# An S4 convolution beside a gated feed-forward: tables by quarters and one half mixed early, in place of tables by halves and one mixing stage

## The chip, the cores and the metric

The kernel runs on one core of one Trainium2 chip. Its time is the device time of one execution in microseconds (us). Five engines work side by side, each through its own list of instructions in a fixed order: TensorE (PE in the profile, with its weight loads as PEld), VectorE (DVE), ScalarE (ACT), GpSimd (POOL) and SyncE (SP). An engine stops at an instruction whose inputs are not there yet, and everything behind it in its list waits with it. SP computes nothing; it issues all the transfers, and it too stops at a transfer that isn't ready.

## The reference

Two branches read the same input x of 2048 rows by 640 channels and are blended by a gate per row.

```python
g = _sigmoid((x * gate_w).sum(-1, keepdims=True))
a = _A_ref(x, ...)         # long convolution, per channel, plus u * Dskip
b = (_gelu(x @ w_gate) * (x @ w_up)) @ w_down      # 640 -> 1728 -> 640
return g * a + (1 - g) * b

# inside _A_ref, D = 640 channels, N = 128 states, L = 2048
P = jnp.exp(logdA[:, :, None] * l[None, None, :])
K = jnp.einsum("dn,dnl,dn->dl", Cc, P, dB).real
y = irfft(rfft(u, 2 * L) * rfft(K, 2 * L))[:L]
```

So the kernel K(d, l) of every channel has to be made first, a sum of 128 complex exponentials; then u and K are transformed, multiplied and transformed back. The branch b is three matrix products.

## The kernel before

**Feed-forward.** Two groups of 1024 rows. For each of 14 slices of the hidden width, `gate` does ten matmuls of 512 columns (line 500) into a pair of PSUM banks and ACT takes the GELU (504); `up` does ten more (520) and DVE multiplies (524). `downs` does 28 matmuls of 320 columns for 128 rows (548) and scales the result into `zt` (245 on ACT, 249 on DVE). PSUM has eight banks and every step takes two, so four steps can be open at a time.

**The tables of K.** K is factored over two grids of time steps. `kgen(q)` fills two tables for a half of 320 channels, q = 0 or 1: `exps1` (599) and `exps2` (627) take exponentials on ACT, 64 and 40 in all over both halves; `phases` makes angles on DVE (580 scales for the first grid, 582 for the second, 584 adds a quarter turn) and sines on ACT (589); `grid1` and `grid2` multiply both on DVE (613, 614, 637). `cs1` and `cs2` exist once, so the second half's exponentials wait until `contract` has read the first half's tables on PE (650). The contraction's output is evicted, re-sorted by `pick` (661) and stored to the scratch `dS`. `gathers` (744, 752) then brings K back from `dS` in 17 strided transfers into `Kl`.

**The transforms.** A transform of length 4096 is split 64 by 32. The first step (128-row matmuls) is line 719 for u and `stageA`, line 780, for K; both store to DRAM scratch, `dU` and `dKA`. The second step reads the scratch by 32 slots in chunks of four (`loadB`) and uses 64-row tiles: `stageB` (807). `swap` makes a copy of U with real and imaginary rows exchanged by two transfers; `mix` runs stage B on K, multiplies both by U (826, 827) and goes back with 834, then stores to `dY`. `finish` loads dY, does the last step (854), adds with the gate's weight into `zt` (859) and stores the output. `evac` is the helper that copies PSUM to SBUF, on ACT (243) or DVE (247).

In this kernel u's second step, `mix` and `finish` run on all 640 channels at once. `stageA` runs by halves. So no chunk of `mix` can begin before K of both halves is made, and no load of `finish` before the last dY store.

**What sets the order.** `Plan.add` records every step with what it reads and writes. `emit` goes through the list `ORDER`; each number holds the step, its engine and its PSUM pair, and each engine gets its instructions in that order. Nothing is decided at run time. The numbers in P, and the durations given to `add`, have no effect on what is emitted.

Of the kernel before, what the change touches and what calls it, by code (L numbers as in the profile page):

```python
# [27 lines left out]
    336 1392 652 276 12 296 356 436 616 476 636 948 516 24 376 416 316 456 496 964 556 536 44 596 1468 576 224 676  # L28
    696 64 896 936 856 2740 1448 876 396 984 6316 796 1484 816 916 836 1408 716 736 1544 2981 2836 776 756 1064 1428
    2862 3076 1004 1024 1044 4383 2956 2768 1124 1084 1104 2888 10580 10604 3008 4404 2782 10636 1508 3020 2804 2856  # L30
    1568 1604 2903 3096 248 3044 88 3101 2976 4428 1664 2602 1148 6320 3196 6348 2624 2924 1168 6362 2656 3220 6436
    6388 1524 1188 6416 3128 3463 3316 3248 4444 3142 1584 3556 3488 1628 3261 3216 3164 1204 6440 1688 3336 6483
    3822 3284 6556 6464 6508 1644 3501 1228 3916 6536 3848 3340 3576 1244 1264 4183 1284 3368 3436 3524 1704 6562
    4208 4276 6600 3581 6676 6588 6628 6656 3703 1724 3608 3676 1304 3622 3728 3796 3940 3696 1324 3644 1348 4061
    4036 104 3968 6683 1364 4156 6722 1944 6796 4088 3860 6748 2004 6708 1748 6776 3981 3936 3884 3382 4056 1828
    1764 4004 1788 4223 3456 3404 1868 1804 4300 4296 1908 1844 4244 128 1924 3741 4376 1884 1968 144 6802 3816 6843
    6916 3764 6828 1984 6868 168 6896 4101 2064 2028 4176 4328 6922 2124 6963 7036 6988 6948 4344 2088 7016 184 4124
    2044 7043 208 7082 7068 4460 2184 7156 7108 2148 7136 2104 2164 2208 9464 7161 7203 4488 4742 7276 7188 2224
    7228 7256 9524 2480 4768 2321 2504 2443 2344 2242 2464 2360 2264 2281 2384 2403 2304 7322 2424 9728 7280 4661
    7396 7304 7344 9768 9744 7376 9808 2523 9784 2560 4684 4502 2588 2544 9848 9824 2716 2736 9408 2696 9864 2676  # L40
    7401 4524 7440 4703 7516 7424 9888 7464 8276 8296 8236 9448 9904 7496 8316 8436 8336 4542 4724 8456 8536 8576
    9388 8416 8356 8396 8496 8476 8556 7521 4564 7560 9428 8256 4583 7636 7584 8376 8516 7544 7616 9488 4622 4604
    9548 9584 7680 7641 4648 9504 4783 7756 7668 7708 7736 4902 4808 4876 9644 5021 9608 4996 9564 7760 5116 7803
    7876 7824 7788 9668 9924 5260 7856 5048 4823 5356 9984 4928 7921 4896 7948 4844 7882 7996 7908 4941 5288 9684
    7976 5142 5016 4964 10008 8003 5236 8040 9624 5061 8116 8068 5136 10104 8028 5300 9948 8096 5383 5376 5324 5168
    10044 8160 5476 5408 8122 8188 5503 5084 8148 8216 9964 5420 5528 5596 9704 10068 5742 10024 5496 5444 8621
    10128 5836 8583 10164 5180 8608 11176 11356 8648 5623 10144 5256 5768 8676 5204 5861 5716 5648 10084 10188 5782
    5956 5540 5804 5856 5888 11536 10204 8723 5616 8682 5564 8708 10221 8748 10262 8776 10244 10300 10284 10343
    10324 10381 10364 8822 10404 8780 8848 10423 8808 10462 8876 10444 11221 11260 10488 11244 11183 11288 11302
    11716 11204 11328 11541 11360 11568 11384 11402 12636 11663 11428 12616 8881 11684 8920 8908 11582 8944 10503  # L50
    11608 11621 10524 10540 11648 12076 8976 5902 10568 12696 12716 10656 10716 10676 11721 11763 5924 11800 11748
    10696 5976 11828 11841 11784 12256 11442 11868 11480 11896 11504 11468 12203 12161 12736 12228 12184 12756 12082
    12120 12656 12108 9023 12144 12676 8981 9048 5982 9004 9076 6080 13076 6008 13036 13056 13116 13096 6163 12976
    6108 13016 12996 12956 12936 12261 12816 12342 6188 12380 12284 12896 12916 12368 12404 12023 12776 12301 12048
    12856 6122 12324 12836 12876 12796 6076 11900 11943 6144 11981 11928 12436 11968 9080 12004 9122 9108 6203 9144
    9176 5661 6224 13120 5684 5736 13162 13148 13363 13188 13260 13384 13321 13288 13222 13216 13344 12443 13248
    12480 12468 12504 12562 13316 9181 13416 12588 12523 9204 6020 12548 13422 6044 13461 13448 13523 13548 13562
    13484 6240 13588 13516 13616 13663 6268 11052 13621 13684 9222 9248 13644 9276 13763 6284 13722 13716 13788
    13748 13861 11064 13823 13888 13816 13844 11088 13916 9280 9322 9304 10721 9348 11112 9376 11124 11148 10843
    10744 13936 14336 14736 10760 10864 13942 13981 10784 14023 13968 14008 14044 14342 14420 14368 14741 14444  # L60
    14783 14768 14062 14804 15136 14860 14088 14381 14404 14888 14463 10882 15576 14488 14104 14504 14124 15260
    15141 10908 15183 15288 14524 15222 16456 15248 14180 15168 14262 14204 15208 14221 14284 14140 14248 14583
    15536 14164 14622 14608 15556 14541 15304 14648 14660 14316 14823 14568 15996 10802 15976 14688 15324 16016
    14848 14716 14904 14924 15381 10828 15420 15623 15408 15582 15444 15608 14941 15644 14968 15020 14982 15048
    15341 15004 15703 15368 15060 15724 15462 15088 16416 15661 16436 15484 15688 10923 15116 16896 15744 15516
    16876 16856 15764 16100 15821 10944 16128 16062 15848 16084 16020 15783 16048 16141 15804 15862 16168 15900
    15884 16503 15928 16581 16184 16528 16462 15956 16540 16488 10963 16568 16204 16608 16624 16644 17022 16220
    10988 16981 16248 16903 17044 17008 16300 16924 16262 16328 16941 16284 16968 16343 16740 16368 16781 17064
    16702 16768 16396 16663 16808 11000 17084 16688 16728 16836 17141 11024 17183 17168 17222 17204 17100 17248
    17124 17276 17436 17296 17576 17716 17481 17443 17504 17996 17464 17302 17340 17556 17324 17536 17364 17856  # L70
    17581 17623 17396 17604 17416 17644 18136 17722 17760 17744 17676 18276 17784 17696 18041 18003 18064 17816
    17836 18024 18116 17862 18096 17900 17884 17924 17956 18141 17976 18183 18164 18204 18282 18236 18320 18256
    18304 18344 18396 18376
# [67 lines left out]
def kernel(  # L141
# [35 lines left out]
    P = dict(sw=2.88, gate=4.41, up=4.47, gelu=8.0, age=1.5, mul=0.68, un=1.47, x2=0.57, uw=-0.09, K0=4.0,  # L177
             K1=5.12, W=5.01, RT=6.05, ua=5.35, ue=5.41, down=6.0, z=2.55, e1=-6.63, e2=-3.06, ph=-4.32,
             gate1=8.05, up1=6.41, gelu1=8.23, gs=3.94, d1=0.43, ct=5.37, T2=5.26, A0=2.9, A1=-10.08, U1=1.18,
             C1=2.96, F1=-0.28)  # L180
# [33 lines left out]
    def mm(n):  # L214
        return n / 2.28 + 4
# [47 lines left out]
    O_CS2 = O_CS1 + 40960  # L263
    O_KST = O_CS2 + 25600
    O_TRIG = O_KST + 2560
    O_PH = O_TRIG + 10240
    O_K2 = O_PH + 20480
    O_UA = O_K2 + 3200

# [9 lines left out]
    cs1 = at(O_CS1, [128, 2, 80, 128], BF16, "cs1")  # L279
    prT = {}  # L280
    names = ("AreT", "AimT", "CreT", "BreT", "CimT", "BimT")
    for i, nm in enumerate(names):
        prT[nm] = at(O_CS2 + 1280 * i, [N, D], BF16, nm)
    ldtT = at(O_CS2 + 7680, [N, D], BF16, "ldtT")
    dtT = at(O_CS2 + 8960, [N, D], BF16, "dtT")
    vr, vi, wt, wm, wq = [at(O_CS2 + 10240 + 2560 * i, [N, D], FP32, nm) for i, nm in enumerate(("vr", "vi", "wt", "wm", "wq"))]
    cs2 = at(O_CS2, [128, 2, 80, 4 * NE], BF16, "cs2")
    trig = [at(O_TRIG + 5120 * k, [128, 2, 80, 16], BF16, f"trig{k}") for k in range(2)]
    phb = [at(O_PH + 10240 * k, [128, 2, 80, 16], I32, f"ph{k}") for k in range(2)]
# [3 lines left out]
    magdt = at(O_A + 7680, [N, D], BF16, "magdt")  # L293
    vrdt = at(O_A + 8960, [N, D], BF16, "vrdt")
    drow = at(O_A + 10240, [128, D], BF16, "drow")[0:1]
    krow = [drow[:, W * h:W * h + W] for h in range(2)]
    kst = at(O_KST, [128, 4 * NE, 80], BF16, "kst")
    kst2 = at(O_K2, [128, 5, 4, 80], BF16, "kst2")
    un = at(O_UA, [128, D], BF16, "un")
    ua = at(O_UA + 1280, [128, 2, D], BF16, "ua")  # L300
    O_TT = O_ZA
    tph = at(O_TT, [128, 2, 512], I32, "tph")
    iot = at(O_TT + 4096, [128, 640], I32, "iot")
    tpb = at(O_TT + 6656, [128, 3, 64], I32, "tpb")

# [250 lines left out]
    def logits(k):  # L556
        for t in range(NPH):
            for kt in range(NKT):
                nc.tensor.matmul(ps[:, k, t:t + 1], lhsT=xT[t // 4][:, kt, 128 * (t % 4):128 * (t % 4) + 128],
                                 rhs=gwc[:, kt:kt + 1], start=(kt == 0), stop=(kt == NKT - 1))  # L560


    RKQ = (P["K0"], P["K1"])
    nph = [0]

    def quads(ap):
# [391 lines left out]
```

## Time and profile before

| what | value |
|---|---|
| median of 3 runs | 327.5 us (326.74 to 327.61) |
| the profiled execution | 327.61 us, its span 325.8 us |
| granted TensorE clock, mean | 0.92 |
| PE busy | 266.1 us, 82% |
| DVE busy | 246.3 us, 76% |
| ACT busy | 223.6 us, 69% |
| weight loads busy | 146.7 us, 45% |
| moved by DMA | 60.57 MB, 57% of 16 engines' span |

A row of an instruction group reads: line, engine, operation, output and input by name, shapes, count, then busy time and mean duration in ns, then the idle time just before and what ended it. A row of the time order begins with the start and the length in us; in square brackets stand the idle time before it and the engine or transfer that ended it. Busy times of neighbours that overlap are counted once. The kernel keeps nearly all its data in one tile, `arena`, so most operands have that name; `ps` is PSUM.

### The profile page before, as it was taken

The numbers are of one execution on the slowest core, as the hardware profiler recorded it, in microseconds if no ns is written. First come the engines' busy times: TensorE is split into PE (matmuls) and PEld (weight loads), VectorE is DVE, ScalarE is ACT, GpSimd is POOL, SyncE is SP. The second block draws the span as 40 slices with busy tenths as digits, with TensorE's granted clock in tenths as the row PEclk, the third lists the DMA queues.
The fourth block names the chain that finished last, engine by engine and source line by source line (L and its number), as shares of the span: only waits on it lengthen the run. The fifth ranks groups of instructions, "written<-read, shape, count | busy, mean of one in ns | idle before, by whom it ended". The sixth has DMA issues, their size and how long they took to land.

```text
span 325.8 us, 5490 instructions
## 1 busy us (share of the span) xinstructions
PE 266.1 (82%) x2112; PEld 146.7 (45%) x2126; DVE 246.3 (76%) x332; ACT 223.6 (69%) x307; POOL 5.3 (2%) x18
## 2 busy tenths in 40 slices
PE   0799999897796999979899987985998889993452
PEld 0254444443366677534344743432465456551220
DVE  4687999999999963799996977254363899982464
ACT  4998997699995599998989576525471386671000
POOL 3000000000000000000000000000110000000000
PEclk9989999999797999999999997999899799998555
DMA  6993344332321144433437659979366569934997
GB/s 171 394 331 104 121 140 125 100 103 81 125 76 42 62 123 130 143 123 120 141 100 240 188 192 291 341 163 260 115 204 221 181 240 330 344 141 163 368 353 245
DMA packets 47519, 60.57 MB, mean 186 GB/s; under 512 B 4419, under 2 KB 41862, under 8 KB 47494
## 3 DMA queue, kind: packets, MB, share of 16 engines
q1 hardware_dynamic: 47494, 60.23, 57.3%
q8 instruction: 16, 0.26, 0.3%
q14 instruction: 9, 0.07, 0.1%
HBM read 35.80 MB, written 19.17 MB: 169 GB/s over the span
## 4 chain that ended last, share of the span: by engine, by line
PE 36%; ACT 22%; DVE 18%; DMA 15%; issue 5%; SPq 3%; DVEq 0%; ACTq 0%
PE ps L548 13%; PE ps L520 8%; PE ps L500 7%; ACT arena L243 6%; ACT arena L589 5%; DVE arena L247 5%; DMA dKA<-arena 4%; ACT arena L599 4%; DMA arena<-dY 3%; DMA arena<-dU 3%; ACT arena L504 3%; DMA arena<-dKA 2%; DVE arena L859 2%; PE ps L650 2%; PE ps L807 2%
## 5 line engine op out<-in xcount | busy, mean ns | idle before, releaser
L243 ACT CAST arena<-ps 128x640 bf16<-128x640 f32 x111 | 70.6, 702 | 38.1 <-PE ps L807 15.7
L500 PE MATMUL ps<-arena 128*128 128x512 bf16 x276 | 66.5, 392 | 13.0 <-DMA arena<-in_u_T_dram 9.2
L247 DVE CAST arena<-ps 128x640 bf16<-128x640 f32 (+2 forms) x67 | 56.2, 881 | 20.1 <-PE ps L807 10.4
L520 PE MATMUL ps<-arena 128*128 128x512 bf16 x250 | 63.1, 401 | 4.2 <-DVE arena L524 1.9
L548 PE MATMUL ps<-arena 128*128 128x320 bf16 x448 | 65.0, 305 | 1.0 <-DVE arena L247 0.5
L548 PEld LDWEIGHTS <-arena 128*128 128x128 bf16 x448 | 44.5, 100 | 20.6 <-issue 2.1
L500 PEld LDWEIGHTS <-arena 128*128 128x128 bf16 x280 | 28.0, 100 | 47.9 <-issue 14.1
L520 PEld LDWEIGHTS <-arena 128*128 128x128 bf16 x260 | 26.5, 103 | 37.2 <-issue 9.3
L589 ACT ACTIVATE arena<-arena 128x2560 bf16<-128x2560 int16 x18 | 41.6, 2334 | 0.4 <-DVE arena L637 0.3
L524 DVE TENSOR_TENSOR arena<-ps,arena 128x1024 bf16<-128x1024 f32 x26 | 31.6, 1218 | 13.1 <-PE ps L520 12.9
L504 ACT ACTIVATE arena<-ps 128x1024 bf16<-128x1024 f32 (+1 forms) x28 | 27.7, 1023 | 9.4 <-PE ps L500 9.2
L807 PE MATMUL ps<-arena 64*64 64x320 bf16 x256 | 16.9, 325 | 9.0 <-DMA arena<-dKA 2.8
L599 ACT ACTIVATE arena<-arena 128x320 bf16<-128x320 f32 x64 | 23.3, 455 | 1.0 <-DVE arena L451 1.0
L854 PE MATMUL ps<-arena 128*64 128x320 bf16 x64 | 10.2, 474 | 14.5 <-DMA arena<-dY 14.5
L859 DVE SCALAR_TENSOR_TENSOR arena<-ps,g_f,arena 128x640 bf16<-128x640 f32 x16 | 13.0, 878 | 11.9 <-PE ps L854 11.9
L249 DVE TENSOR_SCALAR arena<-ps,omg 128x640 bf16<-128x640 f32 x10 | 8.8, 883 | 14.9 <-PE ps L548 14.9
L627 ACT ACTIVATE arena<-arena 128x320 bf16<-128x320 f32 x40 | 14.8, 455 | 5.9 <-PE ps L650 5.9
L582 DVE SCALAR_TENSOR_TENSOR arena<-arena 128x320 int32<-128x320 f32 x40 | 16.9, 483 | 0.8 <-ACT arena L589 0.7
L650 PE MATMUL ps<-arena 128*128 128x80 bf16 x320 | 13.5, 212 | 3.8 <-DVE arena L637 2.8
L807 PEld LDWEIGHTS <-arena 64*64 64x64 bf16 x256 | 8.2, 107 | 17.7 <-issue 9.7
L650 PEld LDWEIGHTS <-arena 128*128 128x128 bf16 x320 | 13.3, 107 | 4.6 <-DVE arena L637 3.5
L780 PE MATMUL ps<-arena 128*128 128x320 bf16 x64 | 12.1, 308 | 4.1 <-DMA arena<-dS 2.3
(93 smaller groups left out, 240.8 us busy)
## 6 DMA issues: line engine op xcount, KB each, us to landing
arena<-in_w_gu_dram SPq DMA_DIRECT2D x52, 160.0 KB, 2.2
dU<-arena SPq DMA_DIRECT2D x16, 320.0 KB, 2.3
arena<-dU SPq DMA_DIRECT2D x8, 640.0 KB, 4.7
dKA<-arena SPq DMA_DIRECT2D x16, 320.0 KB, 4.2
arena<-arena SPq DMA_DIRECT2D x16, 320.0 KB, 4.3
arena<-dKA SPq DMA_DIRECT2D x8, 640.0 KB, 6.0
dY<-arena SPq DMA_DIRECT2D x8, 640.0 KB, 6.1
arena<-dY SPq DMA_DIRECT2D x8, 640.0 KB, 5.6
```

Of the source, the lines that this page charges most:

```text
L243: nc.scalar.copy(out=dst, in_=src(b))
L247: nc.vector.tensor_copy(out=dst, in_=src(b))
L500: nc.tensor.matmul(ps[:, k + j, :], lhsT=Wg[w][:, kt, :], rhs=xT[2 * grp + j][:, kt, :], start=(kt == 0), stop=(kt == NKT - 1))
L504: add({"ACT": an(1024)}, lambda s: nc.scalar.activation(out=HTall[0:p, :, f, :], in_=ps[0:p, plan.bank(g):plan.bank(g) + 2, :], func=ACT.G ...
L520: nc.tensor.matmul(ps[:, k + j, :], lhsT=Wu[w][:, kt, :], rhs=xT[2 * grp + j][:, kt, :], start=(kt == 0), stop=(kt == NKT - 1))
L524: add({"DVE": v1(1024)}, lambda s: nc.vector.tensor_tensor(out=HTall[:, :, f, :], in0=ps[:, plan.bank(u):plan.bank(u) + 2, :], in1=HTall[: ...
L548: nc.tensor.matmul(ps[:, k + h, 0:W], lhsT=HTq[q][:, f, 128 * j:128 * j + 128], rhs=Wd[f][:, W * h:W * h + W], start=(f == 0), stop=(f == ...
L589: ac(an(8 * W), lambda: nc.scalar.activation(out=t[:], in_=ph.bitcast(I16)[:, :, :, 0:32:2], func=ACT.Sin, scale=SIN_SCALE), r=[f"ph{k}"], ...
L599: nc.scalar.activation(out=cs1[:, 1, :, 4 * s:4 * s + 4], in_=quads(aT[:, ds]), func=ACT.Exp, scale=float(sg * (4 + 8 * i)))
L650: nc.tensor.matmul(ps[:, k + i // g, 80 * (i % g):80 * (i % g) + 80], lhsT=cs1[:, x, k0 + i, :], rhs=cs2[:, x, k0 + i, :], start=(x == 0), ...
L807: nc.tensor.matmul(ps[64 * y:64 * y + 64, k + x, 0:W], lhsT=TB[64 * x:64 * x + 64, 0, :], rhs=t[64 * x:64 * x + 64, 2 * a + y, HV[h]], sta ...
L859: add({"DVE": v1(D)}, lambda s, p=p, ph=ph, z=z: nc.vector.scalar_tensor_tensor(out=z, in0=ps[:, plan.bank(p):plan.bank(p) + 2, 0:W], scal ...
```

## The change

The tables are made by quarters of 160 channels, so `kgen` runs four times, `exps1` and `exps2` issue twice as many exponentials of half the length, and `cs1` and `cs2` take half the room. The first grid's angles are one broadcast product for eight steps in place of a scaling for each. `contract` stores to `dS` after every second quarter.

The scratch `dKA` and `dY` is split by halves of the channels. u's second step, the swap, `mix` and `finish` are functions of a half. Half 0 goes through them in eight chunks of four slots right after its own `stageA`, in two sets of buffers; half 1 later in four chunks of eight slots. A dKA store then writes runs of 2560 or 5120 bytes where it wrote 640; loads of dU and dKA and stores of dY and of the output are cut in runs of 640 where they had 1280 or 2560. `finish` runs by halves, four loads each. The first step of u loads two phases at a time and has three output buffers for one. `ORDER` is another list, of 980 steps for 920; PE issues the same products with 64 more instructions and weight loads together, and SP issues 162 transfers for 149.

```diff
--- before.py
+++ after.py
 ORDER = [int(v) for v in """
-    336 1392 652 276 12 296 356 436 616 476 636 948 516 24 376 416 316 456 496 964 556 536 44 596 1468 576 224 676
...
+    12 416 276 296 376 356 636 316 1392 24 576 652 948 476 436 6596 496 336 964 396 556 44 1708 536 616 64 1668 896
...
-    cs1 = at(O_CS1, [128, 2, 80, 128], BF16, "cs1")
+    cs1 = at(O_CS1, [128, 2, 40, 128], BF16, "cs1")
-    cs2 = at(O_CS2, [128, 2, 80, 4 * NE], BF16, "cs2")
-    trig = [at(O_TRIG + 5120 * k, [128, 2, 80, 16], BF16, f"trig{k}") for k in range(2)]
-    phb = [at(O_PH + 10240 * k, [128, 2, 80, 16], I32, f"ph{k}") for k in range(2)]
+    cs2 = at(O_CS2, [128, 2, 40, 4 * NE], BF16, "cs2")
+    trig = [at(O_TRIG + 5120 * k, [128, 2, 40, 32], BF16, f"trig{k}") for k in range(2)]
+    phb = [at(O_PH + 10240 * k, [128, 2, 40, 32], I32, f"ph{k}") for k in range(2)]
...
-    kst = at(O_KST, [128, 4 * NE, 80], BF16, "kst")
-    kst2 = at(O_K2, [128, 5, 4, 80], BF16, "kst2")
-    un = at(O_UA, [128, D], BF16, "un")
-    ua = at(O_UA + 1280, [128, 2, D], BF16, "ua")
+    kst = at(O_KST, [128, 4 * NE, 40], BF16, "kst")
+    kst2 = at(O_KST + 6400, [128, 5, 4, 80], BF16, "kst2")
+    un = at(O_UA, [128, 2, D], BF16, "un")
+    ua = [at(O_UA + 2560 + 2560 * k, [128, 2, D], BF16, f"ua{k}") for k in range(3)]
-    dKA = dp.tile([128, 32, D], BF16, name="dKA")
-    dY = dp.tile([128, 32, D], BF16, name="dY")
+    dKA = [dp.tile([128, 32, W], BF16, name=f"dKA{h}") for h in range(2)]
+    dY = [dp.tile([128, 32, W], BF16, name=f"dY{h}") for h in range(2)]
...
-                if grid == 1:
-                    nc.vector.tensor_scalar(out=o, in0=quads(bK[:, ds]), scalar1=float(4 + 8 * i), scalar2=None, op0=ALU.mult)
+            if grid == 1:
+                nc.vector.tensor_tensor(
+                    out=ph[:, 1].rearrange("p k (i j) -> p k i j", j=4), in0=quads(bK[:, ds])[:, :, None, :].to_broadcast([128, 40, n, 4]),
+                    in1=ci8[:, None, i0:i0 + n, None].to_broadcast([128, 40, n, 4]), op=ALU.mult)
+            else:
+                for j in range(n):
+                    nc.vector.scalar_tensor_tensor(out=ph[:, 1, :, 4 * j:4 * j + 4], in0=quads(bK[:, ds]), scalar=float(X2[i0 + j] + CENTRE),
                                                    in1=quads(phiK[:, ds]), op0=ALU.mult, op1=ALU.add)
...
-        ac(2 * n * an(W), go, r=["aT"], w=[("cs1", i0 // 4)], aset="exp", rank=RKQ[q] + P["e1"])
+        ac(2 * n * an(160), go, r=["aT"], w=[("cs1", i0 // 8)], aset="exp", rank=RKQ[q] + P["e1"])
...
+    def contract(q):
+        h, sub = q // 2, q % 2
-        for k0 in range(0, 80, 12):
+        for k0, n in ((0, 12), (12, 12), (24, 8), (32, 8)):
...
+
+        def pick(k):
+            for c in range(4):
+                for g in range(4):
+                    nc.tensor.matmul(ps[32 * g:32 * g + 32, k + c // 2, 200 * (c % 2):200 * (c % 2) + 200], lhsT=sel[:, c, :],
+                                     rhs=kst.rearrange("p (e j) k -> p e j k", j=4)[:, 5 * g:5 * g + 5, c, :], start=True, stop=True)
+
+        p = pe(16 * 45, pick, r=KK + ["msk"], rank=RC, cr=1.0)
...
+        if sub == 0:
+            return
...
-        for g in range(4):
-            grid1(q, 4 * g)
+        for g in range(2):
+            grid1(q, 8 * g)
         neg1(q)
-        for g in range(5):
-            exps2(q, 4 * g)
-        for g in range(5):
-            grid2(q, 4 * g)
+        for i0, n in ((0, 8), (8, 8), (16, 4)):
+            exps2(q, i0, n)
+        for i0, n in ((0, 8), (8, 8), (16, 4)):
+            grid2(q, i0, n)
         contract(q)
     kgen(0)
+    kgen(1)
...
-        dma(160, lambda ph=ph: nc.sync.dma_start(out=un[:], in_=u_nat[:, ph, :]), w=["un"], rank=P["un"])
+        if ph % 2 == 0:
+            dma(320, lambda ph=ph: nc.sync.dma_start(out=un[:], in_=u_nat[:, ph:ph + 2, :]), w=["un"], rank=P["un"], run=2560)
+        a = nua[0] % 3
+        nua[0] += 1
...
-            dma(160 * G, lambda t=t, g=g: nc.sync.dma_start(out=dKA[:, 2 * G * g:2 * G * (g + 1), W * h:W * h + W], in_=t),
+            dma(160 * G, lambda t=t, g=g: nc.sync.dma_start(out=dKA[h][:, 2 * G * g:2 * G * (g + 1), :], in_=t),
...
+    def u_spec(h, u, us, bi, c, CS, R):
+        (U, un_), (Us, sn) = u, us
+        ks = stageB(loadB(dU[:, :, W * h:W * h + W], [("dU", ph) for ph in range(NPH)], bi, c, CS, R), U, un_, CS, R)
+        for s in range(2):
+            dma(40 * CS, lambda s=s: nc.sync.dma_start(out=Us[s:128:2], in_=U[1 - s:128:2]), r=ks, w=[(sn, s)], rank=R, run=2560)
+
+    def mix(h, u, us, kb, bi, c, CS, keys, R):
+        ks = stageB(loadB(dKA[h][:], keys, bi, c, CS, R), t, tn, CS, R)
+        ve(v2(320 * CS), lambda: nc.vector.tensor_tensor(out=U, in0=U, in1=t, op=ALU.mult), r=ks + SK, w=UK, rank=R - .1)
+        ve(v2(320 * CS), lambda: nc.vector.tensor_tensor(out=Us, in0=Us, in1=t, op=ALU.mult), r=ks, w=SK, rank=R - .1)
...
+        v = dY[h][:].rearrange("(s x) i w -> (x i) s w", x=4)
+        dma(80 * CS, lambda: nc.sync.dma_start(out=v[:, CS * c:CS * c + CS, :], in_=t), r=[(tn, a) for a in range(CS // 2)],
+            w=[("dY", h, c)], rank=R - .2, run=640)
+        return ("dY", h, c)
+
+    def finish(h, keys, rings, R):
+        for g in range(4):
+            s = nua[0] % len(rings)
+            nua[0] += 1
+            t, nm = rings[s]
+            dma(640, lambda t=t, g=g: nc.sync.dma_start(out=t, in_=dY[h][:, 8 * g:8 * g + 8, :]), r=keys,
+                w=[(nm, a) for a in range(4)], rank=R, run=5120)
+            for a in range(2):
+                def go(k, a=a, g=g, t=t):
...
+                    ph = 4 * g + 2 * a + b
+                    add({"DVE": v1(W)}, lambda s, p=p, b=b, ph=ph: nc.vector.scalar_tensor_tensor(
+                        out=zt[ph // 8][:, ph % 8, W * h:W * h + W], in0=ps[:, plan.bank(p) + b, 0:W], scalar=g_f[:, ph:ph + 1],
+                        in1=zt[ph // 8][:, ph % 8, W * h:W * h + W], op0=ALU.mult, op1=ALU.add), r=["g"], w=[(f"zt{ph // 8}", ph % 8)], frees=p, rank=R)
...
-        return [(at(off + size * j, [128, n, w], BF16, f"{nm}{j}"), f"{nm}{j}") for j in range(k)]
+                    out=out4[x, :, 4 * g:4 * g + 4, W * h:W * h + W],
+                    in_=zt[g // 2][64 * x:64 * x + 64, 4 * (g % 2):4 * (g % 2) + 4, W * h:W * h + W]),
+                    r=[(f"zt{g // 2}", 4 * (g % 2) + b) for b in range(4)], rank=R, run=640)
...
-    keys = stageA(0, Kl0, blocks(O_UA + 1280, 4, 2560, 1, "aq", W), 2, P["A0"])
-    kgen(1)
+    aq = [(ua[k].rearrange("p r (h w) -> p (r h) w", h=2), f"ua{k}") for k in range(3)]
+    keys = stageA(0, Kl0, aq, 2, P["A0"])
+    bi4 = blocks(O_R, 4, 2560, 3, "bi")
+    U4 = blocks(O_R + 7680, 4, 2560, 2, "U")
+    S4 = blocks(O_R + 12800, 4, 2560, 2, "Us")
+    K4 = blocks(O_R + 17920, 4, 2560, 2, "kb")
+    y0 = []
+    for c in range(8):
+        u_spec(0, U4[c % 2], S4[c % 2], bi4, c, 4, P["C0"])
+        y0.append(mix(0, U4[c % 2], S4[c % 2], K4[c % 2], bi4, c, 4, keys, P["C0"]))
+    kgen(2)
+    kgen(3)
...
-    bi = blocks(O_CS1 + 79360, 4, 5120, 3, "bi")
-    kb = blocks(O_CS1 + 94720, 4, 5120, 2, "kb")
-    U = blocks(O_CS1, 4, 5120, 8, "V")
-    Us = blocks(O_CS1 + 40960, 4, 5120, 4, "Vs")
-    Kl1 = at(O_CS1 + 61440, [128, NPH, W], BF16, "Kl1")
-    uk = [u_spec(U[c], bi, c, P["U1"]) for c in range(8)]
+    Kl1 = at(O_CS2, [128, NPH, W], BF16, "Kl1")
+    U8 = blocks(O_CS1, 8, 5120, 4, "V")
+    S8 = blocks(O_PH, 8, 5120, 4, "Vs")
+    a8 = blocks(O_TRIG, 8, 5120, 2, "ar")
+    b8 = blocks(O_R, 8, 5120, 2, "bj")
+    K8 = blocks(O_R + 10240, 8, 5120, 2, "kc")
     for c in range(4):
-        swap(U[c], Us[c], uk[c], P["U1"])
-    keys += stageA(1, Kl1, blocks(O_CS1 + 71680, 4, 2560, 3, "ar", W), 2, P["A1"])
-    kb += blocks(O_CS1 + 61440, 4, 5120, 2, "kc")
-    ys = []
-    for c in range(8):
-        if c >= 4:
-            swap(U[c], Us[c % 4], uk[c], P["U1"])
-        ys.append(mix(U[c], Us[c % 4], kb[c % 4], bi, c, uk[c], keys, P["C1"]))
-    finish(ys, blocks(O_CS1, 4, 5120, 4, "as"), P["F1"])
+        u_spec(1, U8[c], S8[c], b8, c, 8, P["U1"])
+    keys = stageA(1, Kl1, a8, 4, P["A1"])
+    y1 = [mix(1, U8[c], S8[c], K8[c % 2], b8, c, 8, keys, P["C1"]) for c in range(4)]
+    a8 += blocks(O_CS2, 8, 5120, 2, "as")
+    finish(0, y0, a8, P["F0"])
+    finish(1, y1, a8, P["F1"])
```

## The prediction

> **What bounds the kernel now.** I read the 40 slices first, then busy time by stretch, then the waits, then the instructions in order of time where a stretch changes character. Of the page's second part:
>
> ```profile
> PE   0799999897796999979899987985998889993452
> DVE  4687999999999963799996977254363899982464
> ACT  4998997699995599998989576525471386671000
> ```
>
> ScalarE (ACT), VectorE (DVE) and TensorE (PE) are all near full until about 200 us. Then ACT falls away, and in the last four slices PE does too. The stretches give sizes (time, PE, PE weight load, DVE, ACT, POOL, granted clock, DMA share, GB/s):
>
> ```profile
> 80.00:100.00 20.00, 14.93 (x77) 8.47 (x77) 19.60 (x30) 19.66 (x19) 0.00 (x0) 0.83 0.25 83
> ...
> 297.00:312.00 15.00, 6.12 (x40) 2.71 (x40) 6.46 (x9) 0.00 (x0) 0.00 (x0) 0.56 0.82 308
> ...
> 312.00:326.00 14.00, 4.10 (x26) 1.65 (x24) 6.58 (x8) 0.00 (x0) 0.00 (x0) 0.50 0.80 279
> ```
>
> From 80 to 100 us DVE and ACT have 19.6 us of 20 and PE 14.9: the K tables (exponentials, sines, products) set the pace. From 297 us PE and DVE wait for transfers. The waits name three places:
>
> ```profile
> PEld L854 <- DMA arena<-dY: 18.7, 8, 9.0
> ...
> ACT arena L627 <- PE ps L650: 5.9, 1, 5.9
> ...
> PE ps L780 <- DMA arena<-dS: 2.3, 2, 1.5
> ```
>
> The last stage waits 18.7 us for dY; ACT waits 5.9 us for the first half's contraction to free the table buffer; stage A of half 1 waits for the gathers. Where the tables end, in ACT's order and then in all engines':
>
> ```profile
> 177.60 2.34 ACT L589 ACTIVATE arena<-arena 128x2560 bf16<-128x2560 int16 x1
> ```
>
> ```profile
> 180.38 1.48 DVE L637 TENSOR_TENSOR arena<-arena 128x2560 bf16<-128x2560 bf16 x1
> ...
> 182.32 4.46 PE L650 MATMUL ps<-arena 128*128 128x80 bf16 x120 [0.49 <-ACT arena L504]
> ...
> 206.07 9.16 SPq L744 DMA_DIRECT2D arena<-dS  x10
> ...
> 220.83 0.43 PE L780 MATMUL ps<-arena 128*128 128x320 bf16 x2 [1.50 <-DMA arena<-dS]
> ```
>
> The last sine ends at 179.94 us, the last table product at 181.86, and the contraction of half 1 starts at 182.32. Its 17 gathers hold the DMA queue from 206.07, and PE starts that half's stage A at 220.83, ending at 238.7. The second mark is the tail:
>
> ```profile
> 294.44 1.58 PE L834 MATMUL ps<-arena 64*64 64x320 bf16 x32
> ...
> 300.74 5.57 SPq L847 DMA_DIRECT2D arena<-dY  x5
> ...
> 304.67 1.28 PE L854 MATMUL ps<-arena 128*64 128x320 bf16 x8 [8.64 <-DMA arena<-dY]
> ...
> 305.54 8.01 DVE L859 SCALAR_TENSOR_TENSOR arena<-ps,g_f,arena 128x640 bf16<-128x640 f32 x10 [8.57 <-PE ps L854]
> ...
> 320.22 1.68 DVE L859 SCALAR_TENSOR_TENSOR arena<-ps,g_f,arena 128x640 bf16<-128x640 f32 x2 [0.71 <-PE ps L854]
> ```
>
> The last mixing matmul ends at 296.02; the last dY store starts at 297.05 and takes 3.20 (the chain); eight loads start at 300.74, the first consumer runs at 304.67, the last DVE operation ends at 321.90, the span at 325.84. The profiled run took 327.61, 1.77 more than its span and 0.1 above the median of 327.5.
>
> **Method.** For each engine I sum its instructions, in its own order, up to a mark, each at the pace of its row when nothing waits; the trace says when before reached that mark, so the difference is idle time. The prices:
>
> ```profile
> L589 ACT ACTIVATE arena<-arena 128x2560 bf16<-128x2560 int16 x18 | 41.6, 2334 | 0.4 <-DVE arena L637 0.3
> ...
> L599 ACT ACTIVATE arena<-arena 128x320 bf16<-128x320 f32 x64 | 23.3, 455 | 1.0 <-DVE arena L451 1.0
> ...
> L582 DVE SCALAR_TENSOR_TENSOR arena<-arena 128x320 int32<-128x320 f32 x40 | 16.9, 483 | 0.8 <-ACT arena L589 0.7
> ...
> L580 DVE TENSOR_SCALAR arena<-arena 128x320 int32<-128x320 f32 x32 | 8.2, 320 | 1.6 <-ACT arena L589 1.6
> ...
> L460 DVE TENSOR_TENSOR arena<-arena 128x640 f32<-128x640 f32 x6 | 4.9, 822 | 0.8 <-ACT arena L475 0.7
> ```
>
> Neighbours overlap, so the pace is below the mean: 32 exponentials of 320 take 11.62 us, 0.363 each; a sine of 2560 follows the last after 2.24. The slope between them, 0.84 ns an element, puts an exponential of 160 at 0.23. DVE: L582 paces at 0.405, and L460 (0.82 for 640 float32) gives 1.05 ns an element: 0.235 for 160, 1.45 for 1280. PE: 0.2165 for an FFN matmul (10 in 2.16), 0.1395 for a down (28 in 3.91), 0.15 stage A, 0.062 and 0.047 stage B forward and back, 0.041 contraction, 0.16 finish.
>
> **Part 1, tables by quarters.** ACT: 208 exponentials of 160 for 104 of 320 is 47.8 for 37.8, +10.1; 30 table loads for 26 at 1.283, +5.1; in all, with 2 us of evictions gone to DVE, 225 becomes 238. DVE: eight broadcast products of 1280 for 32 scalings, 11.6 for 8.2; 80 short L582 for 40, 18.8 for 16.2; 32 final operations at 0.45 for 16 at 0.80, +1.6; shorter mixing products +0.8; evictions the rest: 246.4 becomes 258.3. Up to the last table product DVE's sum grows from 155.5 to 182.0 and ACT's to its last sine from 160.7 to 182.2, because half 0's stages also come ahead of it now: of DVE's 26.5, 6.0 are the new table forms, 4.6 six short mixing products, 15.9 evictions and ups. DVE idled 26.4 us up to 181.86. With the same idle time the tables end at 208.4, **+26.1** for the contraction. Ends: DVE had idled only 12.4 by 100.30 (sum 87.9), which gives 194; and there are three table handovers for one, two more at ACT's 5.9, which gives 220. I take the middle, the row measured over the same stage.
>
> **Part 2, half 0's chain in chunks.** PE has 158.2 us issued ahead of that contraction, against 148.8: half 0's mixing has begun. From contraction to the last stage A of half 1 PE issues 31.1 us (80 contraction, 70 FFN, 68 and 64 stage B, 32 stage A) for 43.3. Before took 56.4, 13 of it idle. Now, between the last pick and the first stage A, PE has 14.7 us (50 FFN, 28 and 40 stage B), and that pair was 26.6 apart before. SP's queue puts a w_gu load, a dKA load, a dY store and three swaps between the dS stores and the gathers; each waits for an eviction about 4 us behind the pick, when the dS stores land anyway. Fifteen gathers at the row's 0.54 to 0.9 us follow, then 3 us of landing: stage A starts some 18 us after the pick, PE stalls 4, and evictions behind the pick cost 1. So 36 for 56.4, **-20.4**. Ends: no stall, -5; the old 26.6, +8. The queue also carries 13 more transfers, about 6 us of issue at 0.45, in between; POOL's does not change. A new wait: stage B of chunk c+2 is evicted into the buffer that chunk c's dY store reads; behind it stand gelus and ups on ACT and DVE, then PE's banks. L832 groups are 6 to 8 us apart on PE and a store lands in about 4, so I add nothing.
>
> Then to the last mixing matmul: 50.6 us issued (168 downs, 40 FFN, 128 and 144 stage B, 24 finish) for 51.2, in 57.3 before, 6.1 idle. Half 1 alone is mixed here, through two buffers, so I keep 6: 56.6, **-0.7**. Ends: no idle, -6, or twice, +6.
>
> **Part 3, the tail.** Only half 1 is left: one dY store, four loads for eight. The store is cut in 640-byte runs now. From its issue: 3.5 store, 0.4, 3.9 first load, 0.9 PE, sixteen operations at 0.45 behind one z (8.1), 3.9 from the last operation to the end: 20.7, plus 1.0 from the last mixing matmul, 21.7 for 29.8: **-8.1**. The two last downs (7.8) lie beside store and load. By stretch, runs of 640 bytes move 203 GB/s at 0.65 share from 224 to 240 us (312 at full share); the loads of dY, in long runs, 300 at 0.86 (349) in 301 to 306 us: 0.34 us a MB, under 1 us for what the tail writes. Ends: 17.5 if DVE hides behind the loads (1.58 each), 26 if outputs in short runs queue ahead.
>
> [...]
>
> **Sum.** 26.1 - 20.4 - 0.7 - 8.1 = -3.1 on 325.8: span 322.7, and 324.5 with the 1.77.
>
> **Rivals.** *Handovers (slower).* The next quarter's exponentials cannot start until the contraction has read the one buffer. For it: the 5.9 us row, now three times. Against: ACT has other evictions queued there. Two more at 5.9 give 336; it decides once the tables end 3 us later than 208.4. *Packed tables (faster).* The short quarters let ACT and DVE overlap as before 100 us: tables at 198, 314. For: both at 98% from 80 to 100. Against: DVE idled 14 more by 182. *Gathers (slower).* SP's queue delays them behind half 0's stores; PE waits the old 26.6: +8, 332. *No tail gain (about even).* Outputs in 640-byte runs fill the DMA engines: tail 26, 329.
>
> **How the numbers follow.** Between 326.5 and 328.5, 0.3% either way, a measurement can't tell a change. My case 0.42, 319 to 329: 0.31 faster, 0.05 even, 0.06 slower. Packed 0.19. Handovers 0.18. Gathers 0.13. No tail gain 0.08, 0.03 of it even. Faster 0.50, same 0.08, slower 0.42. The range reaches the packed case and the handover: 313 to 337.
>
> **What would show it.** Last table product near 208; pick of the last quarter near 213; first stage A of half 1 near 231 with a wait for dS of about 4; last mixing matmul near 301; four dY loads at the end and DVE the last bound. Wrong if ACT shows long waits for the contraction, if PE stands over 8 us at stage A, or if the tables end before 200.

## The result, and the profile after

The changed kernel took 352.7 us in the median of four runs (351.3 to 356.2), the kernel before 327.6. The ratio is 1.077, 95% interval 1.066 to 1.087: slower, and outside the predicted range. Ratios leave out executions over 1.5% slower than the fastest of the same kernel. The profiled execution took 351.31 us, its span 349.5, so what lies around the span (1.8 us) is as before and the 23.7 us are all inside it.

The 40 slices of the kernel after (one is 8.7 us long):

```profile
PE   0889999976699999575479879795899813999971
DVE  4959799989899989854599957845476422599665
ACT  3999998899999899974699934634673506056100
```

The three engines were near full up to 200 us before. Now there are two places where all three fall at once: the 19th and 20th slice (157 to 175 us) and the 33rd and 34th (280 to 297 us). By stretch (time, PE, weight load, DVE, ACT, POOL, granted clock, DMA share, GB/s):

```profile
160.00:172.00 12.00, 3.59 (x73) 2.77 (x71) 4.75 (x5) 4.83 (x5) 0.00 (x0) 0.70 0.22 83
...
280.00:296.00 16.00, 2.77 (x27) 1.44 (x25) 3.34 (x5) 4.35 (x6) 2.09 (x2) 0.64 0.64 241
```

No engine is busy for half of either stretch, and the DMA engines are at 0.22 in the first and 0.64 in the second. So no engine is short of capacity there: something waits. What waits is in the list of waits (total us, times, longest):

```profile
DVE arena L892 <- POOL arena L891: 15.1, 2, 10.2
ACT L894 <- DMA arena<-arena: 14.1, 1, 14.1
POOL arena L891 <- ACT arena L894: 11.5, 1, 11.5
ACT arena L590 <- DMA arena<-arena: 7.2, 2, 4.4
DVE arena L250 <- DMA arena<-arena: 6.1, 2, 3.9
DVE arena L638 <- DMA arena<-arena: 3.6, 1, 3.6
DVE arena L578 <- DMA arena<-arena: 2.3, 1, 2.3
```

There is only one transfer from `arena` to `arena`: the swap (line 819). L590 is the sine of the K tables, L578 an angle, L638 a table product, L894 a sine of the inverse first step's table WAT; none of these reads or writes a byte of the buffers of the swap that it waits for. L250 is the eviction helper. In the profile before, no line of the tables waits for a swap; there the first swap is issued after the last product of the K tables, which ends at 181.86:

```profile
191.67 1.19 SPq L820 DMA_DIRECT2D arena<-arena  x2
```

The first place in order of time:

```profile
159.02 4.97 SPq L819 DMA_DIRECT2D arena<-arena  x2
159.47 3.03 PE L651 MATMUL ps<-arena 128*128 128x80 bf16 x80 [0.18 <-ACT arena L246]
161.11 1.49 DVE L578 TENSOR_TENSOR arena<-arena,ci 128x1280 int32<-128x1280 f32 x1 [2.25 <-DMA arena<-arena]
...
165.62 2.34 ACT L590 ACTIVATE arena<-arena 128x2560 bf16<-128x2560 int16 x1 [4.41 <-DMA arena<-arena]
165.66 1.16 DVE L250 CAST arena<-ps 128x960 bf16<-128x960 f32 x1 [2.20 <-DMA arena<-arena]
...
167.98 1.10 SPq L819 DMA_DIRECT2D arena<-arena  x2
170.71 2.34 ACT L590 ACTIVATE arena<-arena 128x2560 bf16<-128x2560 int16 x1 [2.75 <-DMA arena<-arena]
170.73 2.62 DVE L250 CAST arena<-ps 128x640 bf16<-128x640 f32 x3 [3.91 <-DMA arena<-arena]
171.61 0.59 PE L520 MATMUL ps<-arena 128*128 128x512 bf16 x1 [4.04 <-DVE arena L250]
```

Swap, table work, swap, table work: each waits for the other in turn (SP's queue, before these swaps, 1.7 us for the product L638, 3.9 for the angles L585 and 1.1 for the sine), and PE, which has feed-forward products ready, waits for a PSUM pair that DVE cannot empty. The second place:

```profile
282.45 0.81 DVE L892 TENSOR_SCALAR arena<-arena,sc 128x1024 int32<-128x1024 int32 x1 [4.89 <-POOL arena L891]
...
283.32 1.23 SPq L819 DMA_DIRECT2D arena<-arena  x2
...
291.50 1.28 ACT L894 ACT_TABLE_LOAD   x1 [14.09 <-DMA arena<-arena]
...
294.48 0.48 PE L808 MATMUL ps<-arena 64*64 64x320 bf16 x4 [13.23 <-ACT arena L246]
```

The last swap of half 1 starts as soon as DVE has finished WAT's angles, at 283.26; it takes 7.39 us on the chain; then the sine goes, and the evictions and PE behind it. The marks that the prediction used, after:

```profile
219.73 3.03 PE L651 MATMUL ps<-arena 128*128 128x80 bf16 x80 [0.39 <-ACT arena L246]
...
245.71 0.69 PE L787 MATMUL ps<-arena 128*128 128x320 bf16 x2 [4.78 <-DMA arena<-dS]
...
258.31 2.22 PE L787 MATMUL ps<-arena 128*128 128x320 bf16 x12
...
326.37 1.58 PE L832 MATMUL ps<-arena 64*64 64x320 bf16 x32
```

The contraction of the last quarter starts 11 us later than forecast, the last mixing matmul ends 27 us later (327.95), and the tail takes 21.6 us, as forecast.

### The profile page after: what moved, and what is told of

Its sections match the earlier page's. It is cut to its first block, busy times and chain, and to the rows that moved or that the text cites. A ratio compares the mean times of both kernels' runs of the same rounds, so it can differ in the third digit from the quotient of the medians.

```text
span 349.5 us, 5751 instructions
## 1 busy us (share of the span) xinstructions
PE 268.1 (77%) x2139; PEld 143.1 (41%) x2158; DVE 259.5 (74%) x388; ACT 237.9 (68%) x415; POOL 5.3 (2%) x18
## 5 line engine op out<-in xcount | busy, mean ns | idle before, releaser
L246 ACT CAST arena<-ps 128x640 bf16<-128x640 f32 (+2 forms) x110 | 70.2, 696 | 37.0 <-PE ps L832 23.7
L500 PE MATMUL ps<-arena 128*128 128x512 bf16 x273 | 66.9, 396 | 11.7 <-DMA arena<-in_u_T_dram 9.5
L250 DVE CAST arena<-ps 128x640 bf16<-128x640 f32 (+2 forms) x74 | 58.7, 826 | 22.6 <-PE ps L787 6.2
L548 PE MATMUL ps<-arena 128*128 128x320 bf16 x448 | 65.2, 304 | 2.8 <-DVE arena L524 1.9
L548 PEld LDWEIGHTS <-arena 128*128 128x128 bf16 x448 | 43.8, 99 | 22.7 <-issue 2.6
L590 ACT ACTIVATE arena<-arena 128x2560 bf16<-128x2560 int16 (+1 forms) x20 | 41.9, 2119 | 13.8 <-DMA arena<-arena 7.2
L500 PEld LDWEIGHTS <-arena 128*128 128x128 bf16 x280 | 27.9, 101 | 46.8 <-issue 13.1
L520 PEld LDWEIGHTS <-arena 128*128 128x128 bf16 x260 | 26.4, 104 | 43.2 <-issue 16.2
L504 ACT ACTIVATE arena<-ps 128x1024 bf16<-128x1024 f32 (+1 forms) x28 | 27.7, 1023 | 13.4 <-PE ps L500 13.2
L600 ACT ACTIVATE arena<-arena 128x160 bf16<-128x160 f32 x128 | 29.8, 326 | 0.0
L787 PE MATMUL ps<-arena 128*128 128x320 bf16 x64 | 14.5, 352 | 14.9 <-DVE arena L250 5.3
L583 DVE SCALAR_TENSOR_TENSOR arena<-arena 128x160 int32<-128x160 f32 x80 | 19.8, 316 | 0.0
L628 ACT ACTIVATE arena<-arena 128x160 bf16<-128x160 f32 x80 | 18.9, 324 | 0.9 <-DVE arena L451 0.9
L638 DVE TENSOR_TENSOR arena<-arena 128x2560 bf16<-128x2560 bf16 (+1 forms) x12 | 15.1, 1264 | 4.9 <-DMA arena<-arena 3.6
L252 DVE TENSOR_SCALAR arena<-ps,omg 128x640 bf16<-128x640 f32 x11 | 9.7, 881 | 11.7 <-PE ps L548 11.7
L585 DVE TENSOR_SCALAR arena<-arena 128x1280 int32<-128x1280 int32 (+1 forms) x20 | 15.2, 760 | 0.7
L859 DVE SCALAR_TENSOR_TENSOR arena<-ps,g_f,arena 128x320 bf16<-128x320 f32 x32 | 15.4, 542 | 0.2 <-PE ps L853 0.2
L787 PEld LDWEIGHTS <-arena 128*128 128x128 bf16 x64 | 6.3, 108 | 21.9 <-issue 17.3
```

Of the source, the lines that this page charges most:

```text
L246: nc.scalar.copy(out=dst, in_=src(b))
L250: nc.vector.tensor_copy(out=dst, in_=src(b))
L500: nc.tensor.matmul(ps[:, k + j, :], lhsT=Wg[w][:, kt, :], rhs=xT[2 * grp + j][:, kt, :], start=(kt == 0), stop=(kt == NKT - 1))
L504: add({"ACT": an(1024)}, lambda s: nc.scalar.activation(out=HTall[0:p, :, f, :], in_=ps[0:p, plan.bank(g):plan.bank(g) + 2, :], func=ACT.G ...
L520: nc.tensor.matmul(ps[:, k + j, :], lhsT=Wu[w][:, kt, :], rhs=xT[2 * grp + j][:, kt, :], start=(kt == 0), stop=(kt == NKT - 1))
L548: nc.tensor.matmul(ps[:, k + h, 0:W], lhsT=HTq[q][:, f, 128 * j:128 * j + 128], rhs=Wd[f][:, W * h:W * h + W], start=(f == 0), stop=(f == ...
```

## Experiments

**The theory.** The author took the program's semaphores to be set by a tracker that knows which part of a tile each instruction touches. The swap takes every second partition, `Us[s:128:2]` from `U[1 - s:128:2]`. If the tracker takes such a range for the whole tile, then in a kernel that keeps nearly everything in one tile a swap waits for all earlier work of DVE, ACT and POOL on `arena`, and all later work waits for the swap. The built programs say so: the list of instructions with the semaphores that each waits for has, for the changed kernel,

```
SP  L819 DMACopy arena<-arena 64x1280 [waits DVE_49,DMAHW5_49,Activation_49,Pool_49]
ACT L590 Activation arena<-arena 128x2560 [waits DMAHW6_49,DMAHW5_49]
```

The swap waits for POOL, whose instruction there (an index pattern, line 348) has nothing in its buffers, and the sine for two transfer queues, in which the two transfers of the swap just before it stand. Eleven instructions of the tables wait for swaps in this way without sharing a byte, six of the K tables and five of WAT; declared as six tiles (below) none does. How the tracker comes to this was not looked into. The kernel before has the same transfer (line 820) with the same waits, but there the 16 swaps stand behind the K tables. In the changed kernel eight of half 0's 16 are issued between 159 and 215 us, among the tables of the last two quarters, and the last of half 1's 8 behind WAT's angles. Those eight are the four at the first place above and

```profile
201.46 1.11 SPq L819 DMA_DIRECT2D arena<-arena  x2
...
213.60 1.13 SPq L819 DMA_DIRECT2D arena<-arena  x2
```

**Rivals:** the hand-over of `cs1` and `cs2` between quarters; the gathers and SP's queue.

**1. Contiguous ranges** (e1 both halves, e2 half 0 alone, e3 half 1 alone, e4 the kernel before). One line is altered; the products then pair other rows, while sizes, counts and order stay:

```diff
-nc.sync.dma_start(out=Us[s:128:2], in_=U[1 - s:128:2])
+nc.sync.dma_start(out=Us[64 * s:64 * s + 64], in_=U[64 - 64 * s:128 - 64 * s])
```

> The changed kernel with one line altered: the two swaps of every transformed slot exchange the upper and the lower 64 partitions instead of the even and the odd ones (the products then pair the wrong rows; sizes, bytes, counts and the order of the work are those of the changed kernel). The transfer's partition range is then one contiguous run. Theory (the swap with a stride of two partitions is taken as touching all of the one on-chip tile, so table work waits for swaps and swaps for table work, though they share no byte): the table sines no longer show a DMA as what ended their idle time, the 11 us hole at 161 to 172 us and the 14 us wait of the second-half sines near 283 to 294 us go, and the time falls from 352 to between 322 and 335 us. Rival 1 (the hand-over of the two table buffers between quarters): 348 to 354 us, hole still there. Rival 2 (the gathers and the queue of SP in the last quarter): 345 to 352 us.

> As the run with both, but only the 16 swaps of the first half of the columns are contiguous; the 8 of the second half keep the stride of two. Theory of the false waits: the hole at 161 to 172 us goes, the wait of the inverse table's sines on the second half's swaps (14 us) stays, 333 to 345 us. Rivals: 345 to 354 us.

> The other way round: only the 8 swaps of the second half are contiguous. Theory of the false waits: the wait of the inverse table's sines goes, the hole at 161 to 172 us stays, 336 to 348 us; the gains of this run and of the one with the first half add up to that of both within 5 us. Rivals: 348 to 354 us.

> The kernel before with the same one line altered (contiguous halves, wrong rows paired). There the swaps run after the tables. Theory of the false waits: little to gain, 322 to 328 us. If a stride of two partitions were itself slow as a transfer, this kernel too would gain more than 5 us.

| run | median us | ratio to before (95%) |
|---|---|---|
| e1, both | 336.4 | 1.026 (1.019 to 1.033) |
| e2, half 0 | 342.3 | 1.047 (1.041 to 1.052) |
| e3, half 1 | 350.6 | four runs from 344.0 to 351.2, no interval |
| e4, before | 333.4 | 1.020 (1.013 to 1.027) |

e1 fell by 16 us, and its tables wait for no swap any more. At the first place the sines now run back to back:

```profile
160.15 1.48 DVE L578 TENSOR_TENSOR arena<-arena,ci 128x1280 int32<-128x1280 f32 x1
160.20 1.17 SPq L819 DMA_DIRECT2D arena<-arena  x2
...
162.44 4.60 ACT L590 ACTIVATE arena<-arena 128x2560 bf16<-128x2560 int16 x2
```

That rules out both rivals as the main cause. But the time missed the expected range by a microsecond. e3 gives no clear answer: one run took 344.0 us, inside its range, and three 350.2 to 351.2, though in its profile ACT's 14 us wait is gone. And e4, which should have stayed where it was, lost 6 us. The edit changed something else: contiguous halves land later. The rows of the transfers give size and median time from issue to landing. For the swaps of the kernel before:

```profile
arena<-arena SPq DMA_DIRECT2D x16, 320.0 KB, 4.3
```

For those of e4:

```profile
arena<-arena SPq DMA_DIRECT2D x16, 320.0 KB, 6.9
```

For half 1's of the changed kernel, and then of e1:

```profile
arena<-arena SPq DMA_DIRECT2D x8, 320.0 KB, 7.0
```

```profile
arena<-arena SPq DMA_DIRECT2D x8, 320.0 KB, 11.1
```

So the waits had to be taken away with the transfer left as it was.

**2. More tiles** (e5, e6, e7, e10). The stride of two stays; the one tile is declared as several, so that a swap can only be taken as touching its own. Addresses stay as they were, except in e10.

```diff
-    arena = mp.tile([128, ARENA // 2], BF16, name="arena")
+    CUTS = [0, 105088, 125568, 158208, 178688, 188928, 211968]
+    parts = [mp.tile([128, (b - a) // 2], BF16, name=f"arena{chr(97 + i)}") for i, (a, b) in enumerate(zip(CUTS, CUTS[1:]))]
...
-        v = arena[:, off // 2:(off + size) // 2]
+        i = max(j for j in range(len(parts)) if CUTS[j] <= off)
+        v = parts[i][:, (off - CUTS[i]) // 2:(off + size - CUTS[i]) // 2]
```

e6 has only the cut at half 0's ring, e7 cuts the kernel before around its slots V, and e10 sets apart only what half 1's swaps touch, `cs1` with V and the phase buffers with Vs.

```diff
+    CUTS = [0, 188928, 211968]                  # e6
+    CUTS = [0, 105088, 146048, 211968]          # e7
+    PARTS = ((0, 105088, arena, 0), (105088, 125568, arenab, 0), (125568, 158208, arena, 105088),   # e10
+             (158208, 178688, arenad, 0), (178688, ARENA, arena, 137728))
```

> The changed kernel with the one on-chip tile declared as six tiles at the same addresses (cut at the starts of the cs1 table, of what follows it, of the phase buffers, of the transform's rings and of the first half's slot buffers). Nothing else differs: same swaps with a stride of two partitions, same order, all work kept. Swaps can then only be taken as touching their own tiles. Theory of the false waits: table work no longer waits for swaps, the transfers keep their median landing times of 3.0 and 7.0 us (with contiguous halves they took 3.7 and 11.1), so the time is below the 336 us of the contiguous halves: 324 to 335 us. If the gain of the contiguous halves came from the other kind of transfer and not from the waits, this run stays at 348 to 354 us.

> As the six tiles, but only one cut: the first half's slot buffers are a tile of their own, the rest, with the second half's swaps, stays one tile. Theory of the false waits: the first half's swaps no longer meet the tables, the wait of the inverse table's sines on the second half's swaps stays: 334 to 344 us, like the run with contiguous halves in the first half alone (342).

> The kernel before, with its one on-chip tile declared as three tiles at the same addresses (cut at the start and the end of the cs1 table, over which the transformed slots lie). All work kept. Theory of the false waits: its swaps come after the tables and meet little, 323 to 328 us, within 1% of before. A gain of more than 5 us would say that the kernel before paid for such waits too, and that the change only made them dearer.

> The complement of the one cut: three tiles, the cs1 table with the second half's slots over it, the phase buffers with its swapped slots over them, and all the rest with the first half's swaps in one. All work kept. Theory of the false waits, with the two places independent: the hole at 161 to 172 us stays, the 14 us wait of the inverse table's sines goes; the ratio to before is 1.077 less the 0.044 by which the six tiles beat the one cut, 1.033, so 336 to 341 us. If the first half's delay is made up for behind it, less is gained in one run than in the other and the sum of the two gains misses the 27 us of the six tiles by more than 5.

| run | median us | ratio to before (95%) |
|---|---|---|
| e5, six tiles | 325.4 | 0.993 (0.989 to 0.997) |
| e6, half 0 apart | 339.8 | 1.037 (1.031 to 1.043) |
| e10, half 1 apart | 337.9 | 1.035 (1.030 to 1.040) |
| e7, before in three tiles | 326.4 | 0.995 (0.992 to 0.998) |

Declared as six tiles, the changed kernel is 27 us faster than as one, and 0.7% faster than the kernel before. The order, the transfers and the arithmetic are the same; the swaps land in 3.9 and 7.3 us, a little later than the 3.0 and 7.0 that were expected. In e5 the first place looks like this (lines are 5 later than in the kernel after):

```profile
159.05 1.17 SPq L824 DMA_DIRECT2D arenaf<-arenaf  x2
...
161.29 4.60 ACT L595 ACTIVATE arenac<-arenad 128x2560 bf16<-128x2560 int16 x2
```

The swap is issued 0.03 us from where it was, and the sines start beside it at 161.29 instead of 165.62. By stretch (in the kernel after DVE had 4.75 and ACT 4.83 here):

```profile
160.00:172.00 12.00, 9.02 (x101) 5.29 (x99) 10.31 (x24) 11.97 (x25) 0.00 (x0) 0.89 0.43 152
```

The two places add up. From 1.077, e6 takes 0.040 and e10 0.042, together 0.082; e5 takes 0.084. Each leaves the other's wait standing. From the waits of e6:

```profile
ACT L899 <- DMA arenaa<-arenaa: 13.5, 1, 13.5
```

From the waits of e10 (lines 6 later than after):

```profile
ACT arenaa L596 <- DMA arenaa<-arenaa: 6.8, 2, 4.0
DVE arenaa L256 <- DMA arenaa<-arenaa: 5.7, 2, 3.9
```

e7 shows that the kernel before paid little for its swaps: 0.5%, about 1.5 us.

**3. What is left** (e8, e9, e11). e8 cuts half 0's ring tile three times more and moves half 1's input ring off half 0's buffers; e9 joins the two diffs shown above, six tiles and contiguous halves; e11 keeps one tile and puts real and imaginary rows in blocks of 32 partitions.

```diff
-    CUTS = [0, 105088, 125568, 158208, 178688, 188928, 211968]
-    b8 = blocks(O_R, 8, 5120, 2, "bj")
-    K8 = blocks(O_R + 10240, 8, 5120, 2, "kc")
+    CUTS = [0, 105088, 125568, 158208, 178688, 188928, 196608, 201728, 206848, 211968]
+    b8 = blocks(O_UA, 8, 5120, 2, "bj")
+    K8 = blocks(O_R, 8, 7680, 2, "kc")
```

```diff
-    FIELDS = ((0, 1), (1, 15), (5, 1), (1, 31), ...
+    FIELDS = ((0, 1), (1, 15), (5, 1), (0, 31), ...
...
-        v.tensor_scalar(out=tpb[:, 0, 0:64:2], in0=k2I, ...
-        v.tensor_scalar(out=tpb[:, 0, 1:64:2], in0=tpb[:, 0, 0:64:2], ...
+        v.tensor_scalar(out=tpb[:, 0, 0:32], in0=k2I, ...
+        v.tensor_scalar(out=tpb[:, 0, 32:64], in0=tpb[:, 0, 0:32], ...
...
-            dma(40 * CS, lambda s=s: nc.sync.dma_start(out=Us[s:128:2], in_=U[1 - s:128:2]), ...
+                for y in range(2):
+                    o, i = 64 * y + 32 * s, 64 * y + 32 - 32 * s
+                    nc.sync.dma_start(out=Us[o:o + 32], in_=U[i:i + 32])
```

> The six tiles, with the first half's ring tile cut three times more (input ring, slots, swapped slots, product buffers each a tile) and the second half's input ring moved to the place of the forward transform's buffers, so that no buffer crosses a cut. All work kept. It takes away the false waits that are left inside the first half's own chain and a real one, of the second half's loads on the first half's buffers. If the six tiles already took out what mattered: 322 to 328 us. If the chain is still held by such waits: 315 to 322 us.

> The six tiles with the contiguous swap of the upper and lower 64 partitions (wrong rows paired, all counts as before). No false wait either way; only the kind of transfer differs from the six tiles (325 us). If the 11 us between the six tiles (325) and the contiguous halves alone (336) are the price of the slower transfer (landing 11.1 instead of 7.0 us in the second half), this run takes 332 to 338 us. If they are false waits that the contiguous halves had left, it takes 323 to 328 us.

> One tile again, but the swap is made of contiguous ranges with the right rows: the columns of the forward 64-row table and the rows of the backward ones are re-ordered so that real and imaginary rows lie in blocks of 32 partitions, and each slot is swapped by four transfers of 32 partitions in place of two of 64. All work kept. Theory: no false wait, so at most 336 us as with the contiguous halves, whose transfers are slow. If blocks of 32 land as the stride of two does (7 us in the second half), 325 to 330 us; if as slowly as the halves (11 us), or if SP's 24 more issues of about 0.5 us each come to lie on the path, 332 to 340 us.

e8 took 326.2 us, ratio 0.993 (0.991 to 0.996): nothing more to gain there that these runs can tell. e9 took 334.1 us, 1.019 (1.013 to 1.024). Against e5 that is 2.6%, some 8 us, for the kind of transfer alone; against e1, with no false wait in either, the intervals overlap. So the 11 us between e1 and e5 are, within the error, the price of the slower transfers. The six runs of e11 lie from 333.0 to 339.0 us; the four that a ratio counts have a median of 335.1, about 1.02 of the kernel before, in the slower of its two expected ranges. Its four transfers of 32 partitions land in 7.3 us for 160 KB each in half 1, so the contiguous form does not pay in either shape. Whether the landing or the issues cost it more wasn't separated.

## Why the prediction was wrong, by its own steps

The stages of the forecast, against the changed kernel and the same kernel in six tiles (us; the marks are the start of the last quarter's contraction, the end of half 1's stage A, the end of the last mixing matmul, the end of the span):

| stage | forecast | after | six tiles |
|---|---|---|---|
| to the contraction | 208.4 | 219.7 | 207.4 |
| to the last stage A of half 1 | 36.0 | 40.8 | 40.4 |
| to the last mixing matmul | 56.6 | 67.4 | 55.7 |
| tail | 21.7 | 21.6 | 21.7 |
| span | 322.7 | 349.5 | 325.2 |

The marks of the six tiles come from these rows:

```profile
207.39 3.03 PE L656 MATMUL ps<-arenac,arenab 128*128 128x80 bf16 x80 [0.39 <-ACT arenaf L251]
...
232.82 0.69 PE L792 MATMUL ps<-arenac,arenaa 128*128 128x320 bf16 x2 [4.40 <-DMA arenac<-dS]
...
245.60 2.22 PE L792 MATMUL ps<-arenac,arenaa 128*128 128x320 bf16 x12
...
303.22 0.33 PE L837 MATMUL ps<-arenad,arenaa 64*64 64x320 bf16 x4
```

**The step that failed** is the swap in part 2, which that part moves in among the tables of part 1. The prediction counted it among what SP issues, behind an eviction. Of waits that the change adds it named the table handovers and "a new wait", chunk c's dY store against stage B of chunk c+2: both lie between users of the same buffer. The swap shares no byte with the tables, so it was given no wait in either direction, and part 1 kept the idle time of before. Moved in among the tables and beside WAT, it cost 12.3 us before the last contraction and 11.7 between stage A and the last mixing matmul (after less six tiles, in the table); over the whole span that is 24.3 of the 26.8 us by which the forecast missed. The trace before could not price this, since there the swaps stand behind the tables; but the waits were written in the built program, at the swap's line and at the sine's. The mean granted clock fell with the waits (0.91 after, 0.94 in six tiles); what that adds to the 24.3 us was not separated.

**Part 1, tables by quarters: right.** ACT's busy time was to go to 238 and DVE's to 258.3:

```profile
PE 268.1 (77%) x2139; PEld 143.1 (41%) x2158; DVE 259.5 (74%) x388; ACT 237.9 (68%) x415; POOL 5.3 (2%) x18
```

The 208 short exponentials cost 29.8 and 18.9 us, 48.7 for the 47.8 of the slope between 320 and 2560 elements; 80 short angles cost 19.8 for 18.8:

```profile
L600 ACT ACTIVATE arena<-arena 128x160 bf16<-128x160 f32 x128 | 29.8, 326 | 0.0
...
L583 DVE SCALAR_TENSOR_TENSOR arena<-arena 128x160 int32<-128x160 f32 x80 | 19.8, 316 | 0.0
L628 ACT ACTIVATE arena<-arena 128x160 bf16<-128x160 f32 x80 | 18.9, 324 | 0.9 <-DVE arena L451 0.9
```

With the same idle time as before the contraction was to start at 208.4; without the false waits it starts at 207.4, and DVE was busy 181.5 of the first 207.0 us where the forecast had 182.0 and 26.4 idle. One price lacks its working: 1.05 ns an element does not follow from L460 and L582 (0.82 us for 640 and 0.405 for 320 give 1.3). The operations it priced came out near it all the same, by luck as far as the rows tell: 0.245 us for 160 (eight in 1.96) for 0.235, and 1.48 for 1280 for 1.45.

**Part 2, the chain behind the contraction: the mechanism right, the size off.** The wait for dS at half 1's first stage A is 4.4 us in six tiles for 4. The forecast put the first stage A 18 us behind the pick; it took 20.5 (212.37 to 232.82), and from the first to the last stage A 15.0 for some 13.4. The 36 us came out as 40.4, the only term beside the swap that was over 1 us off; what made each piece longer was not looked into. The next stage, 56.6, took 55.7. SP's count was wrong too: the DMA rows sum to 247 transfers for 239, so 8 more and not 13 (nor 162 for 149), and K comes back in 18 gathers a half, not 17.

**Part 3, the tail: right,** 21.6 and 21.7 for 21.7. What the prediction added for runs of 640 bytes, its own estimate of 0.34 us a MB from 203 GB/s at a share of 0.65 and 300 at 0.86, is under 1 us there, less than these runs can tell.

**The rivals.** *Handovers:* no row of waits in the profile after has an exponential behind a contraction; the range's upper end was built on this mechanism, and the loss came from another. The sign that the prediction gave for it, tables ending over 3 us late, did appear (11 us), so by that sign alone the wrong cause would have been named. *Gathers:* from the pick to the first stage A passed 20.5 us (225.17 to 245.71), 4.8 of it PE's wait for dS, where the rival has 26.6. *Packed tables:* did not come about, 207.4 and not 198. *No tail gain:* the tail was gained. The prediction would have called itself wrong on three signs (ACT waiting long for the contraction, PE over 8 us at stage A, tables before 200); none appeared, while the marks that it hoped for were missed (contraction 11 us late, last mixing matmul near 328 for 301). So the list of signs had the same hole as the sum.

## What to carry to other kernels

Before pricing a transfer at its issue and its landing, look at which semaphores the built program makes it wait for, and which instructions wait for it: in a kernel with one big tile, a range with a stride over partitions can order work that shares no byte (352.7 us here as one tile, 325.4 as six). A move that puts such a transfer among other work must be charged for that work stopping, and the cure here was to declare the same bytes as several tiles. When all engines fall at once (and here, in the first place, the DMA share too, to 0.22), look for a wait before looking for a lack of capacity.

## What the runs showed of the hardware

Contiguous halves of 64 partitions were slower to copy inside SBUF than every second partition in transfers of 320 KB, with the same bytes in the same two transfers per slot: 6.9 us to land for 4.3 in the kernel before, and 11.1 for 7.0 in the second half of the changed one. The landing of the stride of two varied with the program around it: without the false waits it took 5.0 us in e7 (the kernel before) and 7.3 in e5 (half 1), where contiguous halves took 11.1 in e9:

```profile
arenac<-arenab SPq DMA_DIRECT2D x16, 320.0 KB, 5.0
```

```profile
arenad<-arenab SPq DMA_DIRECT2D x8, 320.0 KB, 7.3
```

```profile
arenad<-arenab SPq DMA_DIRECT2D x8, 320.0 KB, 11.1
```

For half 0's swaps of 160 KB the two forms hardly differed in tiles, 3.9 us in e5 and 4.0 in e9; in one tile contiguous halves took 3.7 in e1 for 3.0 in the changed kernel. Contiguous halves cost the kernel before 2.0% and the six tiles 2.6%. So for 320 KB the landing took 1.5 to 1.6 times as long, and for 160 KB from about the same to 1.2 times. What makes the contiguous form slower was not shown by any run.
